# Products of a recurrence's decays on GpSimd, their normalisation queued behind a state update

## The chip, the cores and the metric

The kernel runs on one core of a Trainium2 chip. The metric is the time of one execution in microseconds. The engines are named as in the profile: PE (TensorE), DVE (VectorE), ACT (ScalarE), POOL (GpSimd), and SP, which here issues the DMAs.

## The reference

```python
state = np.zeros((B, H, D, D))            # B 4, H 8, S 768, D 40
for t in range(S):
    y[:, :, t] = einsum('bhd,bhde->bhe', rt, state)
    Sa = einsum('bhde,bhe->bhd', state, at)
    state_decay = state * wt[:, :, None, :] - einsum('bhd,bhe->bhde', Sa, bt)
    state = state_decay + einsum('bhd,bhe->bhde', vt, kt)
x = y as (B, S, H * D)
x = _moe_ref(x)      # 4 experts of causal attention, the top 2 of each position
x = _moe2_ref(x)     # a token mixer and a channel mixer
```

The change concerns the recurrence alone, and in it the decays `w`, which lie between 0.85 and 0.95. `_moe_ref` and `_moe2_ref` are left as they are.

## The kernel before

The recurrence (class `Rec`) is computed in chunks of 64 steps, 12 in all, which go in 6 pairs, numbered 0 to 5. The 32 heads lie in G = 11 groups of three heads with 40 partitions each, so that most tiles have 120 partitions.

For a pair of chunks `decay(p)` builds running products of the decays. Each chunk has two halves of 32 steps. The tile `pq` holds the products from the start of a half (`pt`) and those from its end (`qt`). Both are built by the same 31 multiplications (L164), each of 120x88 numbers and each reading what the one before has written. Then come the product of a whole half (`wp`, L166), its reciprocal (L168) and two multiplications that normalise `pt` and `qt` (L171). Two tiny products `f` for the state's decay run on GpSimd (L174, L176).

`scale(p)` multiplies `a` by `pt` (L182), issues the DMAs that spread `a` into `abd`, and multiplies the two halves of `kb` by `qt` (L186). `ptt(p, q)` has PE transpose `pt` (L265). `scores` multiplies blocks of `kb` and `abd` on PE and masks them on DVE (L210). From their diagonal blocks `solve(p)` inverts triangular matrices: a transpose into `tp` (L226), 31 steps of two dependent DVE operations (L235, L237), and a transpose into `xt` (L240). PE reads `xt` in `xz` (L302). `ds` updates the state in four pieces, whose last operation is on DVE (`ST`, L333).

The tiles `w` and `pq` exist once each: the decays of the next pair can be loaded only when those of this one have been read, and `pq` can be written only when the last reader of the pair before is done.

The order in the program is written out by hand. `first()` follows the list `FIRST`; each later chunk follows `EVEN` or `ODD`, in which a letter stands for a step (`S` the solve, `D` the decay of the pair after next, `M` its scaling). The solves and, for pairs 2 to 5, the decays are generators in a queue `s.bg`, from which `s.pump(n)` takes n steps after each step of the list. `tc.issue_after(x)` makes the scheduler put what is in it behind the instruction x on its engine. The scheduler then fixes the order on each engine.

Of the kernel before, what the change touches and what calls it, by code (L numbers as in the profile page):

```python
# [19 lines left out]
F32 = mybir.dt.float32  # L20
# [5 lines left out]
OP = mybir.AluOpType  # L26
AX = mybir.AxisListType
PSUM = bass.MemoryType.PSUM
G = 11
HP = 3  # L30
E = 40
FIRST = "p0 S p1 p2 k0 k1 k2 X L D M V q0 q1 q2"
SPIN = 28
PN = (1, 1)
EVEN = "m2 v0 h0 c0 z0 v1 c1 r0 c2 D v2 z2 x2 c3 m0 c4 x0 t2 z1 y0 x1 t1 c5 t0 h1 r1 r2 x3 y1 h2 c6 c7 k0 x5 c8 s0 c9 y2 x4 c10 c11 s2 d0 m1 S L d2 s1 k1 k2 d1"
ODD = "A z0 x0 v0 v1 z1 z2 r0 h0 x2 t0 m1 x1 m2 s0 v2 r1 y0 h1 m0 r2 M y1 p0 L p1 p2 h2 y2 x3 t1 t2 d0 s2 k0 x5 s1 k1 x4 d2 k2 d1"
QUADS = [(0, 4), (4, 8), (8, 11)]
# [15 lines left out]
def nheads(g):  # L53
    return 2 if g == G - 1 else 3
# [15 lines left out]
class Rec:  # L70
# [76 lines left out]
    def decay(s, p):  # L147
        nc, wk, t = s.nc, s.wk, s.T[p]

        pq = s.ek.tile([120, 2, G, 2, 64], F32, name="pq", bufs=1)
        wp = wk.tile([120, G, 2, 2], F32, name="wp")
        e = nc.vector
        pt, qt, n, x = pq[:, 0], pq[:, 1], 4 * G, 128 * G
        wv, pv, qv = (z.rearrange("p g c (h t) -> p (g c) h t", h=2) for z in (t["w"], pt, qt))

        def two(z, o, step):
            return bass.AP(tensor=z.tensor, offset=z.offset + o, ap=[z.ap[0], [step, 2], [32, n]])

        e.memset(two(pq, 0, x + 31), 1.0)  # L161
        for i in range(31):
            yield
            e.tensor_tensor(two(pq, i + 1, x + 29 - 2 * i), two(t["w"], i, 31 - 2 * i),  # L164
                            two(pq, i, x + 31 - 2 * i), OP.mult)
        e.tensor_tensor(wp.rearrange("p g c h -> p (g c) h"), wv[:, :, :, 31], pv[:, :, :, 31], OP.mult)  # L166
        wr = wk.tile([120, G, 2, 2], F32, name="wr")
        e.reciprocal(wr, wp)  # L168
        rv = wr.rearrange("p g c h -> p (g c) h")
        for z, h in ((pv, 0), (qv, 1)):  # L170
            e.tensor_tensor(z[:, :, h], z[:, :, h], rv[:, :, h:h + 1].to_broadcast([120, 2 * G, 32]), OP.mult)  # L171

        f = wk.tile([120, 2, G], F32, name="f")
        nc.gpsimd.tensor_tensor(f[:, 1, :], wp[:, :, 0, 1], wp[:, :, 1, 0], OP.mult)  # L174
        if p:
            nc.gpsimd.tensor_tensor(f[:, 0, :], s.T[p - 1]["wp"][:, :, 1, 1], wp[:, :, 0, 0], OP.mult)  # L176
        t.update(pt=pt, qt=qt, wp=wp, f=f)
# [130 lines left out]
    def ds(s, c, q, pre):  # L308

        nc = s.nc  # L310
        g0, g1 = QUADS[q]
        kbt, vu = s.T["kbt", c], s.T["vu", c]
        f = s.T[(c + 1) // 2]["f"][:, (c + 1) % 2]
        if pre:
            mf = s.wk.tile([120, 4, 120], F32, name="mf", bufs=3)
            for g in range(g0, g1):
                nc.scalar.activation(mf[:, g - g0], s.bdm, AF.Copy, scale=f[:, g:g + 1])
            s.T["mf", q] = mf
            return
        mf = s.T["mf", q]  # L320
        ps = s.ps.tile([128, 512], F32, name="pm")
        for g in range(g0, g1):
            k = 40 * nheads(g)
            o = 120 * (g - g0)
            nc.tensor.matmul(ps[:k, o:o + k], kbt[:, 120 * g:120 * g + k], vu[:, 120 * g:120 * g + k],  # L325
                             start=True, stop=False)
            nc.tensor.matmul(ps[:k, o:o + k], s.S[:k, g, :k], s.ident[:k, :k], is_transpose=True,
                             start=False, stop=True)
        for gg in ([(g0, g1)] if g1 < G else [(g0, g1 - 1), (g1 - 1, g1)]):
            k = 40 * nheads(gg[1] - 1)  # L330
            l, m = gg[0] - g0, gg[1] - g0
            pv = ps[:k, :480].rearrange("p (g d) -> p g d", d=120)[:, l:m, :k]
            nc.vector.tensor_tensor(s.ST[:k, gg[0]:gg[1], :k], pv, mf[:k, l:m, :k], OP.mult)  # L333

    def st(s, q):
        nc = s.nc
# [85 lines left out]
    def first(s):  # L422

        nc = s.nc
        s.load_w(0)
        s.load_a(0)
        kb = s.ek.tile([120, G, 2, 128], F32, name="kb")
        s.T[0]["kb"] = kb
        src = s.in_kb[0].rearrange("p g c x t -> p g c (x t)")
        for c in range(2):  # L430
            nc.sync.dma_start(kb[:, :, c], src[:, :, c])
        s.consts()
        s.bg = [s.decay(0)]
        s.pump(1000)
        t = s.T[0]
        a, p, q = t["a"], t["pt"], t["qt"]
        e = nc.vector
        for c in range(2):
            e.tensor_tensor(a[:, :, c], a[:, :, c], p[:, :, c], OP.mult)
            s.abd_load(c, (s.abd, s.rbd)[c][0])  # L440
            for x in range(2):
                kbx = kb[:, :, c, 64 * x:64 * x + 64]
                e.tensor_tensor(kbx, kbx, q[:, :, c], OP.mult)
        s.load_chunk(0)
        s.load_r(0)
        for c in range(2):
            for u in range(6):
                s.scores(c, u)

    def run(s):  # L450
        n = s.np
        s.first()

        def loads():
            s.load_w(1)
            s.load_a(1)
            s.load_kb(1)

        def all(f):
            for _ in f:  # L460
                pass

        def decay():
            with s.tc.issue_after(s.solved.ins):
                all(s.decay(1))

        do = dict(S=lambda: all(s.solve(0)), p=lambda q: s.ptt(0, q), L=loads, D=decay,
                  M=lambda: s.scale(1), q=lambda q: s.ptt(1, q), V=lambda: s.load_chunk(1),
                  k=lambda q: s.kbt(0, q), X=lambda: s.spin(s.T['sc', 1], SPIN))
        for o in FIRST.split():  # L470
            if n > 1 or o[0] not in "LDMq":
                do[o[0]](*map(int, o[1:]))
        s.bg = []
        for c in range(2 * n):
            s.chunk(c)
        with s.tc.issue_after(s.solved.ins):
            for _ in s.cv:
                pass
        for q in range(3):
            s.vut(2 * n - 1, q)  # L480
            s.rs(2 * n - 1, q)
            s.hh(2 * n - 1, q)
            s.yy(2 * n - 1, q)
# [9 lines left out]
    def chunk(s, c):  # L493
        n = s.np
        p = c // 2
# [47 lines left out]

        def decay():
            if even and p2:
                s.bg.append(s.decay(p + 2))

        def scale():
            if not even and p2:
                while "pt" not in s.T[p + 2]:  # L550
                    s.pump(1)
                s.scale(p + 2)

        if even and p2:
            s.load_w(p + 2)
# [596 lines left out]
```

## Time and profile before

| | us |
|---|---|
| median of 3 runs | 1045.84 (1043.87 to 1049.55) |
| profiled execution | 1045.46 |
| its span in the trace | 1043.7 |
| PE busy | 959.1 |
| DVE busy | 674.4 |
| ACT busy | 479.3 |
| GpSimd busy | 167.7 |

The span is what the trace covers; 1.8 us lie outside it. A busy time is the sum of an engine's instructions; one that is not the bound can be idle at no cost. The recurrence takes the first 410 us or so.

### The profile page before, as it was taken

How to read it: one execution, taken by the hardware profiler on the slowest of the kernel's cores; microseconds unless marked ns; L12 is line 12 of the kernel's file. 1: busy time of each engine (PE TensorE's matmuls, PEld its weight loads, DVE VectorE, ACT ScalarE, POOL GpSimd, SP SyncE). 2: the span in 40 equal slices, each digit the busy share in tenths (PEclk: the TensorE clock that was granted, in tenths of full speed). 3: DMA queues.
4: the chain of work that ended last, by engine and by line, in shares of the span. 5: the costliest groups of instructions: out<-in, count | busy, mean ns of one | idle time of the engine just before them, and what ended most of it. 6: DMA issues, size and time to landing. Idle time of an engine off the chain costs nothing.

```text
span 1043.7 us, 23515 instructions
## 1 busy us (share of the span) xinstructions
PE 959.1 (92%) x9313; PEld 823.1 (79%) x9313; DVE 674.4 (65%) x1793; ACT 479.3 (46%) x1250; POOL 167.7 (16%) x214
## 2 busy tenths in 40 slices
PE   2977997999999999966999999999998999999998
PEld 1646876888888898855877888888787898898987
DVE  6598898887989685747898777566287222222222
ACT  1324544656665665534677667666543121121211
POOL 5000000010000000352234132223255000000000
PEclk9977996999999999979999999999999999999999
DMA  8604422417253323455543441420262101101000
GB/s 172 138 1 96 100 67 74 111 41 170 53 123 74 86 61 117 157 165 145 154 116 99 118 115 31 96 65 26 87 205 63 56 1 56 39 18 57 1 26 26
DMA packets 101031, 88.84 MB, mean 85 GB/s; under 512 B 60785, under 2 KB 91073, under 8 KB 100321
## 3 DMA queue, kind: packets, MB, share of 16 engines
q1 hardware_dynamic: 100921, 87.34, 32.2%
q8 instruction: 74, 1.21, 0.5%
q14 instruction: 36, 0.29, 0.1%
HBM read 54.94 MB, written 15.73 MB: 68 GB/s over the span
## 4 chain that ended last, share of the span: by engine, by line
PE 66%; DVE 19%; DMA 6%; ACT 4%; issue 3%; POOL 1%; SPq 1%; DVEq 0%; ACTq 0%; POOLq 0%
PE pq L1045 12%; PE p L1059 11%; PE psc L205 4%; PE zu L289 3%; PE psc L387 3%; DVE pq L164 3%; PE po L872 3%; PE pq L846 3%; PE zu L302 2%; PE pq L998 2%; PE pm L325 2%; PE zu L276 2%; DVE x L237 2%; PE y L400 2%; DVE pr L235 2%
## 5 line engine op out<-in xcount | busy, mean ns | idle before, releaser
L1049 DVE SCALAR_TENSOR_TENSOR hl<-pq,hh 128x512 fp32r<-128x512 f32 x72 | 49.7, 690 | 153.6 <-ACT hh L1048 153.6
L1048 ACT ACTIVATE hh<-pq 128x512 fp32r<-128x512 f32 x72 | 42.9, 596 | 186.7 <-PE pq L1045 186.7
L1059 PE MATMUL p<-c2h,hh 128*128 128x320 f32 x288 | 90.8, 315 | 0.0
L819 ACT ACTIVATE a<-s,nm 128x512 f32<-128x512 f32 (+3 forms) x128 | 68.7, 542 | 46.4 <-DVE nm L816 21.6
L1059 PE MATMUL p<-c2l,hh 128*128 128x320 f32 x288 | 89.4, 311 | 0.2 <-POOL c2l L635 0.2
L1059 PE MATMUL p<-c2h,hl 128*128 128x320 f32 x288 | 89.5, 311 | 0.1
L306 ACT ACTIVATE vu<-zu 32x240 f32<-32x240 f32 (+1 forms) x144 | 48.8, 339 | 55.2 <-PE zu L302 45.1
L293 ACT ACTIVATE zt<-zu 32x240 f32<-32x240 f32 (+1 forms) x144 | 48.7, 338 | 51.7 <-PE zu L289 49.6
L814 DVE TENSOR_REDUCE nm<-s 128x1 f32<-128x512 f32 (+3 forms) x128 | 62.0, 500 | 15.7 <-PE s L813 10.8
L164 DVE TENSOR_TENSOR pq<-w,pq 120x88 f32<-120x88 f32 x186 | 61.2, 329 | 9.7 <-DMA w<-in_w 5.8
L832 POOL TENSOR_TENSOR a<-a,rs 128x128 f32<-128x128 f32 (+1 forms) x64 | 45.6, 734 | 126.6 <-DVE rs L827 84.5
L235 DVE TENSOR_TENSOR pr<-tp,x 128x31 f32<-128x31 f32 (+15 forms) x186 | 63.0, 339 | 3.8 <-DVE tp L226 0.5
L237 DVE TENSOR_TENSOR x<-x,pr 128x31 f32<-128x31 f32 (+15 forms) x186 | 63.2, 340 | 3.3
L289 PE MATMUL zu<-vu,sc 64*32 64x40 f32 (+1 forms) x1536 | 61.3, 220 | 1.2 <-ACT vu L306 1.2
L302 PE MATMUL zu<-zt,xt 64*32 64x40 f32 x1536 | 48.3, 211 | 12.5 <-DVE pq L161 6.8
L1045 PE MATMUL pq<-uh,c1h 128*128 128x512 f32 x144 | 57.6, 400 | 0.8 <-DVE ul L666 0.8
L289 PEld LDWEIGHTS zu<-vu,sc 64*32 64x32 f32 (+1 forms) x1536 | 53.2, 127 | 6.2 <-ACT vu L306 2.9
L1059 PEld LDWEIGHTS p<-c2h,hh 128*128 128x128 f32 x288 | 54.5, 189 | 3.7 <-DVE o L1062 1.2
L1045 PE MATMUL pq<-uh,c1l 128*128 128x512 f32 x144 | 57.1, 396 | 0.0
L1059 PEld LDWEIGHTS p<-c2l,hh 128*128 128x128 f32 x288 | 54.5, 189 | 2.9 <-POOL c2l L635 0.5
L387 PE MATMUL psc<-rbd,vut 120*128 120x192 f32 (+1 forms) x264 | 54.6, 341 | 1.9 <-DVE sr L391 1.6
L302 PEld LDWEIGHTS zu<-zt,xt 64*32 64x32 f32 x1536 | 40.3, 117 | 20.1 <-issue 12.8
(206 smaller groups left out, 2504.4 us busy)
## 6 DMA issues: line engine op xcount, KB each, us to landing
kb<-in_kb SPq DMA_DIRECT2D x5, 1320.0 KB
kh<-hb SPq DMA_DIRECT2D x64, 96.0 KB
cv<-in_c SPq DMA_DIRECT2D x18, 256.0 KB
w<-in_w SPq DMA_DIRECT2D x6, 660.0 KB
a<-in_a SPq DMA_DIRECT2D x6, 660.0 KB
r<-in_r SPq DMA_DIRECT2D x12, 330.0 KB
rbd<-in_r SPq DMA_DIRECT2D x36, 110.0 KB
vu<-in_v SPq DMA_DIRECT2D x12, 320.0 KB
```

Of the source, the lines that this page charges most:

```text
L164: e.tensor_tensor(two(pq, i + 1, x + 29 - 2 * i), two(t["w"], i, 31 - 2 * i), two(pq, i, x + 31 - 2 * i), OP.mult)
L235: v.tensor_tensor(prv, tp[:, j + 1:, j:j + 1].to_broadcast([128, n, j + 1]), x[:, j:j + 1, :j + 1].to_broadcast([128, n, j + 1]), OP.mult)
L237: v.tensor_tensor(x[:, j + 1:, :j + 1], x[:, j + 1:, :j + 1], prv, OP.subtract)
L289: nc.tensor.matmul(zu[o:o + m, 40 * i:40 * i + 40], sc[r, h, 32 * half:32 * half + m], vu[r, 40 * h:40 * h + 40], start=False, stop=True, ...
L302: nc.tensor.matmul(zu[o:o + 32, 240 + 40 * i:280 + 40 * i], xt[r, h, :], s.zt[half][r, 40 * h:40 * h + 40], start=True, stop=True, skip_gr ...
L306: nc.scalar.activation(vu[d:d + 32, o:o + n], zu[b + 32 * half:b + 32 * half + 32, 240:240 + n], AF.Copy)
L387: nc.tensor.matmul(ps[:, n:n + nheads(g), :], vt[:k, g - g0, :], rbd[:k, g, :nheads(g), :], start=True, stop=True)
L814: nc.vector.tensor_reduce(nm[:, x:x + 1], s, axis=AX.X, op=OP.max, negate=True)
L819: nc.scalar.activation(a[:, n0:n1], s, AF.Exp, bias=nm[:, -1:] if nb_ == 2 else nm[:, :1], accum_out=sm[:, x, i % 2:i % 2 + 1])
L1045: nc.tensor.matmul(p, l, r, start=(n == 0), stop=(n == 7))
L1049: nc.vector.scalar_tensor_tensor(hl, p, 0.0, hh, op0=OP.max, op1=OP.subtract)
L1059: nc.tensor.matmul(Y[s][i], hs[x][:, ts], w[:, k], start=(k + n == 0), stop=(k == 11 and n == 2))
```

## The change

For pairs 1 to 5 the memset of `pq` and the 31 products run on GpSimd; pair 0 keeps them on DVE. What followed them in `decay(p)` is a function of its own, `norm(p)`, still on DVE. For pair 1 the products are issued without a wait on the solve; `norm(1)` and `scale(1)` stand behind `xt` of the first solve, as the whole of `decay(1)` did. For pairs 2 to 5 the products are issued at once at `D`, not step by step, and `norm` and `scale` come at `M` in the odd chunk, behind the last state update of the even chunk (`s.moved`).

```diff
--- before.py
+++ after.py
@@ -150,19 +150,26 @@
         pq = s.ek.tile([120, 2, G, 2, 64], F32, name="pq", bufs=1)
-        wp = wk.tile([120, G, 2, 2], F32, name="wp")
-        e = nc.vector
-        pt, qt, n, x = pq[:, 0], pq[:, 1], 4 * G, 128 * G
-        wv, pv, qv = (z.rearrange("p g c (h t) -> p (g c) h t", h=2) for z in (t["w"], pt, qt))
+        e = nc.gpsimd if p else nc.vector
+        n, x = 4 * G, 128 * G
...
+        t["pq"] = pq
         e.memset(two(pq, 0, x + 31), 1.0)
         for i in range(31):
             yield
             e.tensor_tensor(two(pq, i + 1, x + 29 - 2 * i), two(t["w"], i, 31 - 2 * i),
                             two(pq, i, x + 31 - 2 * i), OP.mult)
+
+    def norm(s, p):
+        nc, wk, t = s.nc, s.wk, s.T[p]
+        pq = t["pq"]
+        wp = wk.tile([120, G, 2, 2], F32, name="wp")
+        e = nc.vector
+        pt, qt = pq[:, 0], pq[:, 1]
+        wv, pv, qv = (z.rearrange("p g c (h t) -> p (g c) h t", h=2) for z in (t["w"], pt, qt))
         e.tensor_tensor(wp.rearrange("p g c h -> p (g c) h"), wv[:, :, :, 31], pv[:, :, :, 31], OP.mult)
...
-            nc.vector.tensor_tensor(s.ST[:k, gg[0]:gg[1], :k], pv, mf[:k, l:m, :k], OP.mult)
+            s.moved = nc.vector.tensor_tensor(s.ST[:k, gg[0]:gg[1], :k], pv, mf[:k, l:m, :k], OP.mult)
...
         s.pump(1000)
+        s.norm(0)
...
         def decay():
+            all(s.decay(1))
+
+        def scale():
             with s.tc.issue_after(s.solved.ins):
-                all(s.decay(1))
+                s.norm(1)
+                s.scale(1)
...
-                  M=lambda: s.scale(1), q=lambda q: s.ptt(1, q), V=lambda: s.load_chunk(1),
+                  M=scale, q=lambda q: s.ptt(1, q), V=lambda: s.load_chunk(1),
...
         def decay():
             if even and p2:
-                s.bg.append(s.decay(p + 2))
+                for _ in s.decay(p + 2):
+                    pass
 
         def scale():
             if not even and p2:
-                while "pt" not in s.T[p + 2]:
-                    s.pump(1)
-                s.scale(p + 2)
+                with s.tc.issue_after(s.moved.ins):
+                    s.norm(p + 2)
+                    s.scale(p + 2)
```

Three places in the order of the engines. The first is DVE at the head, behind the first solve's `xt`: here the rows of before, from the normalisation of pair 1 on, where the products in them are already those of pair 2.

```order
L171 TENSOR_TENSOR pq<-pq,wr 120x22x32 x2
L182 TENSOR_TENSOR a<-a,pq 120x1408
L186 TENSOR_TENSOR kb<-kb,pq 120x22x64 x2
L161 MEMSET pq 120x2x44
L164 TENSOR_TENSOR pq<-w,pq 120x2x44
L333 TENSOR_TENSOR ST<-pm,mf 120x480
L164 TENSOR_TENSOR pq<-w,pq 120x2x44
L333 TENSOR_TENSOR ST<-pm,mf 120x240
L164 TENSOR_TENSOR pq<-w,pq 120x2x44
L333 TENSOR_TENSOR ST<-pm,mf 80x80
L164 TENSOR_TENSOR pq<-w,pq 120x2x44 x11
L333 TENSOR_TENSOR ST<-pm,mf 120x480
```

And the same place after the change (L247 is the line of `xt`, L173 to L178 are those of `norm`, L189 and L193 of `scale`, L340 of `ST`, L217 of the masked scores).

```order
L247 STREAM_TRANSPOSE xt<-x 128x32x32
L173 TENSOR_TENSOR wp<-w,pq 120x44
L175 RECIPROCAL wr<-wp 120x44
L178 TENSOR_TENSOR pq<-pq,wr 120x22x32 x2
L189 TENSOR_TENSOR a<-a,pq 120x1408
L193 TENSOR_TENSOR kb<-kb,pq 120x22x64 x2
L340 TENSOR_TENSOR ST<-pm,mf 120x480
L340 TENSOR_TENSOR ST<-pm,mf 120x240
L340 TENSOR_TENSOR ST<-pm,mf 80x80
L217 TENSOR_TENSOR sc<-psc,mask 128x384 x4
L340 TENSOR_TENSOR ST<-pm,mf 120x480
```

No product is left on DVE there: `xt` is followed by `wp`, and the state updates by scores.

The second place is DVE around the end of the solve of pair 1. Before:

```order
L237 TENSOR_TENSOR x<-x,pr 128x3x29
L210 TENSOR_TENSOR sc<-psc,mask 128x384
L235 TENSOR_TENSOR pr<-tp,x 128x60
L164 TENSOR_TENSOR pq<-w,pq 120x2x44
L237 TENSOR_TENSOR x<-x,pr 128x2x30
L210 TENSOR_TENSOR sc<-psc,mask 128x128
L235 TENSOR_TENSOR pr<-tp,x 128x31
L164 TENSOR_TENSOR pq<-w,pq 120x2x44
L237 TENSOR_TENSOR x<-x,pr 128x31
L166 TENSOR_TENSOR wp<-w,pq 120x44
L240 STREAM_TRANSPOSE xt<-x 128x32x32
```

And after (L242 and L244 are the two operations of a solve's step, L233 is the transpose `tp` of the next pair's solve).

```order
L242 TENSOR_TENSOR pr<-tp,x 128x60
L244 TENSOR_TENSOR x<-x,pr 128x2x30
L242 TENSOR_TENSOR pr<-tp,x 128x31
L244 TENSOR_TENSOR x<-x,pr 128x31
L233 STREAM_TRANSPOSE tp<-td 128x1024
L247 STREAM_TRANSPOSE xt<-x 128x32x32
L242 TENSOR_TENSOR pr<-tp,x 128x31
L244 TENSOR_TENSOR x<-x,pr 128x31
```

The products between the solve's operations are gone, and the next pair's `tp` stands ahead of `xt`; the scores lie earlier.

The third place is GpSimd after the change, from the `f` of pair 0 on, with what each row waits for (L160 and L163 are the memset of `pq` and the products, L130 a memset of `vu`, L235 and L236 those of the solve's `x`, L181 and L183 the `f`).

```order
L181 TENSOR_TENSOR f<-wp 120x11 [waits DVE_49]
L130 MEMSET vu 64x1280 [waits Pool_49]
L235 MEMSET x 128x1024 [waits Pool_49]
L130 MEMSET vu 64x1280
L236 MEMSET x 128x32 [waits Pool_49]
L160 MEMSET pq 120x2x44 [waits DVE_49,PE_49]
L163 TENSOR_TENSOR pq<-w,pq 120x2x44 [waits DMAHW6_49,Pool_49]
L163 TENSOR_TENSOR pq<-w,pq 120x2x44 [waits Pool_49] x30
L130 MEMSET vu 64x1280 [waits Pool_49]
L235 MEMSET x 128x1024 [waits DVE_49,Pool_49]
L181 TENSOR_TENSOR f<-wp 120x11 [waits DVE_49]
```

The products of pair 1 now stand on GpSimd behind the memsets for the first chunks, and wait for the readers of pair 0's `pq` and for the load of `w`.

## Rows read from the trace of the kernel before

**Rows 1.** The page, section 4: shares of the chain that ended last, by engine.

```profile
PE 66%; DVE 19%; DMA 6%; ACT 4%; issue 3%; POOL 1%; SPq 1%; DVEq 0%; ACTq 0%; POOLq 0%
PE pq L1045 12%; PE p L1059 11%; PE psc L205 4%; PE zu L289 3%; PE psc L387 3%; DVE pq L164 3%; PE po L872 3%; PE pq L846 3%; PE zu L302 2%; PE pq L998 2%; PE pm L325 2%; PE zu L276 2%; DVE x L237 2%; PE y L400 2%; DVE pr L235 2%
```

**Rows 2.** Waits of PE, total us, times, longest.

```profile
PE pm L265 <- DVE pq L171: 5.6, 1, 5.6
PE zu L302 <- DVE xt L240: 4.9, 3, 3.8
```

**Rows 3.** Busy time by stretch: start:end and length, then PE, PEld, DVE, ACT, POOL.

```profile
85.00:120.00 35.00, 33.72 (x442) 28.84 (x440) 29.99 (x62) 21.13 (x53) 1.54 (x3) 0.92 0.53 124
...
150.00:166.00 16.00, 7.69 (x55) 5.44 (x52) 15.68 (x53) 3.18 (x5) 0.39 (x2) 0.79 0.32 90
...
185.00:216.00 31.00, 29.71 (x462) 26.53 (x458) 27.63 (x75) 18.41 (x53) 2.32 (x2) 1.00 0.38 88
...
250.00:283.00 33.00, 31.38 (x439) 28.00 (x438) 29.14 (x82) 17.22 (x47) 2.32 (x2) 0.95 0.33 78
```

**Rows 4.** Timeline of DVE at the head: start, us, operation.

```profile
69.73 1.90 DVE L240 STREAM_TRANSPOSE xt<-x 128x1024 f32<-128x1024 f32 x1
...
71.81 11.17 DVE L164 TENSOR_TENSOR pq<-w,pq 120x88 f32<-120x88 f32 x31
...
85.36 1.62 DVE L182 TENSOR_TENSOR a<-a,pq 120x1408 f32<-120x1408 f32 x1
```

**Rows 5.** Timeline of PE at the head; in brackets idle time before and releaser.

```profile
76.96 2.10 PE L302 MATMUL zu<-zt,xt 64*32 64x40 f32 x47
84.70 2.52 PE L265 MATMUL pm<-ident,pq 120*128 120x120 f32 x11 [5.63 <-DVE pq L171]
```

**Rows 6.** Timeline of DVE between pair 0's scaling and the first solve.

```profile
23.47 1.69 DVE L443 TENSOR_TENSOR kb<-kb,pq 120x704 f32<-120x704 f32 x2
...
46.33 0.21 DVE L235 TENSOR_TENSOR pr<-tp,x 128x31 f32<-128x31 f32 x1 [0.50 <-DVE tp L226]
```

**Rows 7.** Two stretches behind PE's restart, as rows 3; the granted clock follows POOL.

```profile
85.00:91.00 6.00, 5.98 (x28) 4.85 (x27) 5.51 (x6) 3.21 (x7) 0.00 (x0) 0.51 0.62 152
91.00:94.00 3.00, 3.00 (x33) 2.71 (x32) 2.13 (x7) 1.39 (x5) 0.00 (x0) 1.00 0.02 6
```

**Rows 8.** Groups of DVE in 125 to 164.2: count, busy us, mean ns.

```profile
L164 DVE TENSOR_TENSOR pq<-w,pq 120x88 f32<-120x88 f32 x26 | 8.6, 331 | 0.0
```

**Rows 9.** Timeline of DVE near the end of pair 1's solve.

```profile
161.47 0.31 DVE L164 TENSOR_TENSOR pq<-w,pq 120x88 f32<-120x88 f32 x1
161.69 0.24 DVE L235 TENSOR_TENSOR pr<-tp,x 128x87 f32<-128x87 f32 x1
```

**Rows 10.** Groups of POOL by shape: count, busy us, mean ns.

```profile
L580 POOL TENSOR_TENSOR sc<-sc 128x512 f32<-128x512 f32 x6 | 8.0, 1331 | 48.7 <-DVE sc L579 47.4 <-PE y L357 1.3
...
L832 POOL TENSOR_TENSOR a<-a,rs 128x128 f32<-128x128 f32 x16 | 6.5, 409 | 82.9 <-DVE rs L827 69.6 <-ACT hb L781 5.2 <-ACT a L819 4.9
...
L174 POOL TENSOR_TENSOR f<-wp 120x11 f32<-120x11 f32 x6 | 1.2, 207 | 87.1 <-DVE wp L166 40.5 <-ACT zt L293 23.3 <-ACT S L348 12.3
```

**Rows 11.** Timeline of all engines where weights are split, behind the recurrence.

```profile
454.39 0.29 DVE L574 TENSOR_SCALAR cv<-cv 128x256 int32<-128x256 int32 x1 [2.02 <-DMA cv<-in_c]
...
454.73 2.08 POOL L635 TENSOR_TENSOR t1l<-cv,t1h 128x768 fp32r<-128x768 f32 x1 [2.76 <-ACT t1h L634]
...
455.17 1.78 DVE L577 TENSOR_SCALAR cv<-cv 128x256 int32<-128x256 int32 x1
...
457.45 0.49 DVE L666 TENSOR_TENSOR xl<-pq,xh 128x128 fp32r<-128x128 f32 x2
457.50 0.73 POOL L580 TENSOR_TENSOR cv<-cv 128x256 f32<-128x256 f32 x1 [0.69 <-DVE cv L579]
```

**Rows 12.** Groups of DVE in 170 to 214.7, most of pair 2's solve.

```profile
L164 DVE TENSOR_TENSOR pq<-w,pq 120x88 f32<-120x88 f32 x12 | 4.0, 335 | 0.0
```

**Rows 13.** Groups of DVE in 240 to 282.2, most of pair 3's solve.

```profile
L164 DVE TENSOR_TENSOR pq<-w,pq 120x88 f32<-120x88 f32 x13 | 4.3, 329 | 0.0
```

**Rows 14.** Timeline of PE at its first use of pair 3's xt.

```profile
284.30 1.09 PE L302 MATMUL zu<-zt,xt 64*32 64x40 f32 x42 [0.49 <-DVE pq L164]
```

## Prediction

> **What bounds the kernel now.** I read the chain that ended last first [rows 1]: PE holds 66% of it and DVE 19%, and the decay products of L164 appear in it under a name of their own with 3%. Next the list of what PE waits for [rows 2]: one wait of 5.6 us is on the normalised decays, and the waits on xt add up to 4.9 us. Then the stretches [rows 3]. In most of the recurrence PE is busy for nearly the whole stretch (29.71 of 31 us, 31.38 of 33). There are two places where it isn't: the head, where pair 1's decays are built, and 150 to 166, where PE works 7.69 of 16 us while DVE works 15.68. Everything behind 410 us is the mixture of experts and the channel mixer, which the change doesn't touch.
>
> So a microsecond taken off DVE is worth a microsecond in those two places, and little elsewhere until DVE falls behind.
>
> **The change part by part.**
>
> *Head.* Between the solve's transpose xt(0), which ends at 71.63, and the normalisation DVE spends 11.2 us on the 31 products of pair 1 [rows 4]. PE finishes its own work at 79.06 and sits idle to 84.70, released by the normalisation [rows 5]. After the change DVE goes from xt(0) straight to wp. From the last product to the end of the normalisation is 2.4 us (82.98 to 85.36), so PE's transposes could start at about 74, and PE has work until 79. The idle 5.6 us goes. GpSimd must have the products ready at 71.6. It may write pq only when the scaling of pair 0 has read it, by about 25 us, and until the solve begins at 46.3 DVE has only scores, whose input is in PSUM [rows 6]. With 13 us for the products (below) they end near 39, before the solve, and even at 22 us near 47. I cost them at nothing; without that cover they would slow the solve, as below.
>
> The idle stretch also has a price behind it. In 85:91 PE is busy throughout at half speed (a granted clock of 0.51), and from 91 it has full speed [rows 7]. If the idle stretch goes, the clock may be back before this work. Matmuls that are bound by the clock would then take half of the 6 us, a gain of 3.0 at most; nothing is the other end. I take 2.0, nearer the top since PE is busy throughout that row. Head: −7.6 us.
>
> *Products of pair 2.* They lie between the state updates and scores of 90 to 106; PE idles 1.3 us in 85:120 in all [rows 3]. I take −0.8 (0 to −1.3). GpSimd starts them when pair 1 is scaled, about 79 (w(2) can be loaded once wp of pair 1 has read w(1), near 72), and ends about 92; the normalisation stands on DVE behind the last state update, which DVE reaches at about 94. What is queued behind it are chunk 3's scores. The price of late products there is their lateness less the 5.0 us that DVE idles in 85:120 [rows 3].
>
> *Solve of pair 1* (the long DVE stretch to 166). Of the products 26 lie between 125 and 164 [rows 8]. One product between two solve operations costs the queue not its 0.33 us but what lies from its start to that of the next operation, 0.22 to 0.26 (161.47 to 161.69 [rows 9]), since they overlap: 26 × 0.245 = 6.4 us go. Against it, the next pair's transpose tp, which stands behind xt now, comes before it in the new order; as one of xt's kind it takes 1.9 us [rows 4]: +2.0.
>
> *What GpSimd's products do to DVE.* No row shows 120x88 on GpSimd. The bounds are a 120x11 product of 0.207 us and a 128x128 one of 0.409 [rows 10]; a line from the first to the second gives 0.34 at 88, one from the first to 128x512 (1.33) gives 0.38. I take 0.36, with 0.06 between dependent instructions: 13 us for 31, bounds 6.5 and 15 (22 if two runs of strided data cost as much again). The other price is that of meeting DVE. While GpSimd ran a 768-wide product for 2.08 us, a DVE operation on 128x256 took 1.78, where another of its kind and size just before took 0.29 [rows 11]: it waited for nearly all that was left of the product. Both read SBUF. Two DVE operations with an input in PSUM, just behind, take 0.49 together beside a product of GpSimd, and don't look stretched. The solve's two operations per step, the scaling and the normalisation have all inputs in SBUF. If each product that meets the solve holds back one operation, it costs 0.36 − 0.06 = 0.30 us. The Trainium skill says so outright ("SBUF — State Buffer", section "Who interferes with whom"): a VectorE instruction with two SBUF inputs and a GpSimd instruction that reads SBUF exclude each other, and the second one is fully blocked. By it the price is the 0.30 taken here; if GpSimd were free of DVE, the price would be nothing. The trace's pair of 2.08 and 1.78 us agrees with the page.
>
> Pair 3's products run on GpSimd from about 108 to 121, and meet the solve of pair 1 in their last 11: +3.3 (0 to +5). The solve of pair 1 thus comes to −6.4 + 2.0 + 3.3 = −1.1 (−4.4 to +0.6).
>
> *Solves of pairs 2 and 3.* Here 12 and 13 products lie between solve operations [rows 12] and [rows 13]; without them −6.1 us together. But GpSimd's products for the next pair now start when the earlier scaling has let go of pq, and fall on the solve: I count 22 meetings in the one (it is one third over) and all 31 in the other: 53 × 0.30 = +15.9. DVE is idle 3.4 us of 31 and 3.9 of 33 [rows 3], which takes up some: 15.9 − 6.1 − 7.3 = +2.5 us. That the rest is felt at once is in the rows: PE takes up xt(3) at 284.30, having waited 0.49 us for DVE [rows 14]. I take +3.0, for what doesn't spread evenly; bounds 0 (products of 0.21 us: 53 × 0.15 = 8, less than 13.4) and +5 (products of 0.41). In pair 4 no products are left, and the normalisation and scaling come into the solve: nothing.
>
> *Moved.* The normalisation and scaling are queued behind the even chunk's last state update, not among the pumped steps; their 2.3 and 4.8 us on DVE are the same. The load of w(4) moves behind kb(3) on SP, 60 us ahead of its use. Both nothing.
>
> **Sum.** −7.6 − 0.8 − 1.1 + 3.0 = −6.5 us on the profiled execution's 1045.46 gives 1039.0; that execution is 0.4 below the median of the runs.
>
> **Rivals.**
> - *No contention* (chance 0.20): GpSimd and DVE don't hinder each other here. For it: no row shows these shapes together. Against: the stretched operation of [rows 11]. Then the solve of pair 1 is −4.4, pairs 2 and 3 nothing: −7.6 − 0.8 − 4.4 = −12.8, or 1032.7.
> - *The gain is eaten* (0.22): products near 0.45 us. The meetings cost 53 × 0.39 = 20.7, less 13.4 is +7.3; pair 1 +0.6. −7.6 − 0.8 + 0.6 + 7.3 = −0.5, or 1045.0: no change that can be told.
> - *GpSimd becomes the bound* (0.13): strided products take 0.6 us or more. Then pairs 2 and 3 pay 53 × 0.54 = 28.6 less 13.4 = +15.2, PE waiting at both xt, and the solve of pair 1 +1: −7.6 − 0.8 + 1.0 + 15.2 = +7.8, or 1053.3. It decides from 0.48 us for a product, where the meetings eat the head's gain. For it: the products' rows are of one run each, and these have strides and two runs. Against: the 120x11 form is strided too and costs 0.207; at the 2.6 ns an element of the 1.33 us form, 88 elements add 0.23 to that.
> - *The forecast* (0.45): 1039.0.
>
> **How the numbers follow.** About 0.5%, 5.2 us, is what measurement can tell. The forecast's own range is 1035 to 1042; the range over the cases, 1030 to 1048, leaves out most of the third rival and the far end of the first. Faster by over 0.5% (under 1040.6): all of the first rival, 0.36 of the forecast's 0.45, little of the second: 0.58. Same: 0.28. Slower: 0.14.
>
> **What would show it.** After the change: PE has no wait on the normalised decays near 80, and the clock is at full speed before 85 (head). xt(1) ends near 156, with a wait before L302 of some 3 us left. A GpSimd product takes 0.34 to 0.37 us, more where it meets the solve; the solve's operations have means above 0.34 us in pairs 2 and 3, and PE waits 1 to 4 us for xt(2) or xt(3). Wrong would be: solve operations of unchanged means (first rival), products of 0.5 us and more (third), or a normalisation on DVE that waits for GpSimd.

## The result, and the profile after

The changed kernel takes 1056.62 us in the median of 16 runs (1043.22 to 1064.09), the kernel before 1044.55. The ratio is 1.0079 (1.0055 to 1.0102): 0.8% slower, where 0.6% faster was forecast and the range ended at 1048. It leaves out the slowest five of the 16 runs; the two medians by themselves lie 1.2% apart. The profiled execution has a span of 1052.7 us.

First the engines' busy times and the GpSimd products on the page of the changed kernel (L163 is their line).

```profile
PE 970.1 (92%) x9313; PEld 829.5 (79%) x9313; DVE 644.8 (61%) x1633; ACT 480.9 (46%) x1250; POOL 250.2 (24%) x374
...
L163 POOL TENSOR_TENSOR pq<-w,pq 120x88 f32<-120x88 f32 x155 | 80.1, 517 | 12.5 <-DMA w<-in_w 0.4
```

DVE lost 30 us of work and GpSimd gained 82. PE has exactly as many matmuls as before and is busy 11 us longer (959.1 before): the same matmuls took longer. The span less this busy time is 84.6 us before and 82.6 after, so in this pair of executions all of the 9 us is longer matmuls and none of it more waiting. A product on GpSimd takes 0.517 us, not 0.36. Next the waits of PE on DVE that answer to [rows 2].

```profile
PE zu L309 <- DVE xt L247: 8.4, 4, 7.0
PE zu L309 <- DVE wp L173: 6.9, 1, 6.9
PE y L364 <- DVE ptt L411: 3.8, 2, 2.8
```

The 5.6 us on the normalised decays are gone, as forecast. The waits for xt, 4.9 us before, are 8.4, and 7.0 of that is xt(1) (3.8 before), which was to be early. The 6.9 us under `wp` are the wait for xt(0), put down to the operation that DVE does next; before, the same 6.8 us stand under the memset of `pq`, so [rows 2] leaves them out. Now the stretches, as in [rows 3] and [rows 7].

```profile
72.00:79.00 7.00, 7.00 (x95) 5.58 (x95) 4.44 (x3) 3.89 (x10) 2.13 (x5) 0.50 0.50 111
...
85.00:88.00 3.00, 3.00 (x18) 3.00 (x17) 0.66 (x1) 0.66 (x4) 2.61 (x6) 0.50 0.00 0
88.00:91.00 3.00, 3.00 (x23) 2.16 (x21) 0.55 (x2) 1.86 (x5) 2.61 (x6) 0.77 0.04 8
...
352.00:365.00 13.00, 13.00 (x129) 10.84 (x122) 2.99 (x6) 4.70 (x14) 0.00 (x0) 0.51 0.48 96
```

At the head PE now works from 69.7 us without a wait longer than 0.43 us, yet at half speed until about 89. Before, it waited 5.6 us there and had full speed from 91; in both the clock came back 19 to 20 us after PE took up xt(0). And behind xt(4) there are 13 us of full work at half speed, a stretch that the trace of before has at full speed (its mean granted clock from 342 to 375 is 1.00). By half of the 13 us, an estimate, about 6.5 us are lost there alone. Where it begins, PE's timeline shows this.

```profile
345.97 0.57 PE L349 MATMUL pm<-ident,ST 120*120 120x120 f32 x4
347.20 0.42 PE L349 MATMUL pm<-ident,ST 120*120 120x120 f32 x2 [0.66 <-ACT S L355]
...
349.50 0.69 PE L309 MATMUL zu<-zt,xt 64*32 64x40 f32 x21 [0.45 <-DVE xt L247]
350.85 0.51 PE L296 MATMUL zu<-vu,sc 64*32 64x40 f32 x13 [0.31 <-ACT vu L313]
```

Three short waits follow one another, for ACT, for xt(4) and again for ACT. In the order of before PE had only the waits of 0.43 and 0.31 us there; the 0.66 us is new, and matmuls of scores and outputs that stood behind xt(4) now lie ahead of it.

Why is xt(4) late? From tp(4) at 300.60 to xt(4) at 347.50 are 46.9 us, against 40.5 before (300.26 to 340.80), though no product is left in this solve. DVE's timeline shows the new entries.

```profile
308.67 0.33 DVE L244 TENSOR_TENSOR x<-x,pr 128x175 f32<-128x175 f32 x1
311.50 1.63 DVE L193 TENSOR_TENSOR kb<-kb,pq 120x1408 f32<-120x1408 f32 x1 [2.50 <-DMA kb<-in_kb]
...
347.50 1.95 DVE L247 STREAM_TRANSPOSE xt<-x 128x1024 f32<-128x1024 f32 x1
349.48 0.66 DVE L411 TENSOR_TENSOR ptt<-y,ptt 64x240 f32<-64x240 f32 x2
```

The normalisation of pair 5 stood ahead of tp(4) before; now it lies in the solve, 2.3 us. The whole solve stands behind the scaling, which waits 2.50 us for the load of kb (1.24 before). And the scheduler has put one `sc`, four `sr` and four `ptt` operations ahead of xt(4) that came behind it before.

Last, the run-to-run spread. The 16 runs of the changed kernel lie between 1043.2 us at a mean granted clock of 0.969 and 1064.1 at 0.948, on a line of 8.6 us per 0.01 (a fit over the 16). The median clock is 0.956; that of 91 runs of the kernel before, made with the experiments below, is 0.965. At 0.965 the line gives 1048.9 us, and the like line of before 1045.2. So of 11.6 us between the medians of all these runs some 8 go with the lower granted clock, and 4 are the rest.

### The profile page after: what moved, and what is told of

The parts are those of the page before. It is cut to its first block, busy times and chain, and to the rows that moved or that the text cites. A ratio compares the mean times of both kernels' runs of the same rounds, so it can differ in the third digit from the quotient of the medians.

```text
span 1052.7 us, 23516 instructions
## 1 busy us (share of the span) xinstructions
PE 970.1 (92%) x9313; PEld 829.5 (79%) x9313; DVE 644.8 (61%) x1633; ACT 480.9 (46%) x1250; POOL 250.2 (24%) x374
## 4 chain that ended last, share of the span: by engine, by line
PE 66%; DVE 18%; DMA 7%; ACT 5%; issue 3%; POOL 1%; SPq 1%; DVEq 0%; ACTq 0%; POOLq 0%
PE pq L1058 11%; PE p L1072 11%; PE psc L212 5%; PE psc L394 3%; PE zu L309 3%; PE zu L296 3%; PE pq L859 3%; PE po L885 3%; DVE pr L242 3%; DVE x L244 2%; PE pm L332 2%; PE pq L1011 2%; PE y L407 2%; DMA kb<-in_kb 2%; PE pq L1024 2%
## 5 line engine op out<-in xcount | busy, mean ns | idle before, releaser
L163 POOL TENSOR_TENSOR pq<-w,pq 120x88 f32<-120x88 f32 x155 | 80.1, 517 | 12.5 <-DMA w<-in_w 0.4
L313 ACT ACTIVATE vu<-zu 32x240 f32<-32x240 f32 (+1 forms) x144 | 48.9, 339 | 56.0 <-PE zu L309 52.1
L827 DVE TENSOR_REDUCE nm<-s 128x1 f32<-128x512 f32 (+3 forms) x128 | 62.0, 500 | 15.9 <-PE s L826 11.6
L242 DVE TENSOR_TENSOR pr<-tp,x 128x31 f32<-128x31 f32 (+15 forms) x186 | 67.7, 364 | 5.8 <-POOL x L236 1.3
L244 DVE TENSOR_TENSOR x<-x,pr 128x31 f32<-128x31 f32 (+15 forms) x186 | 67.4, 362 | 3.9
L217 DVE TENSOR_TENSOR sc<-psc,mask 128x384 f32<-128x384 f32 x72 | 36.0, 511 | 47.2 <-PE psc L212 45.9
L309 PE MATMUL zu<-zt,xt 64*32 64x40 f32 x1536 | 49.9, 214 | 15.8 <-DVE xt L247 8.4
L309 PEld LDWEIGHTS zu<-zt,xt 64*32 64x32 f32 x1536 | 41.2, 119 | 26.0 <-issue 14.6
```

The lines of the kernel that those rows point to most:

```text
L242: v.tensor_tensor(prv, tp[:, j + 1:, j:j + 1].to_broadcast([128, n, j + 1]), x[:, j:j + 1, :j + 1].to_broadcast([128, n, j + 1]), OP.mult)
L244: v.tensor_tensor(x[:, j + 1:, :j + 1], x[:, j + 1:, :j + 1], prv, OP.subtract)
L309: nc.tensor.matmul(zu[o:o + 32, 240 + 40 * i:280 + 40 * i], xt[r, h, :], s.zt[half][r, 40 * h:40 * h + 40], start=True, stop=True, skip_gr ...
L313: nc.scalar.activation(vu[d:d + 32, o:o + n], zu[b + 32 * half:b + 32 * half + 32, 240:240 + n], AF.Copy)
L827: nc.vector.tensor_reduce(nm[:, x:x + 1], s, axis=AX.X, op=OP.max, negate=True)
```

## Experiments

The theories. **A**: short waits of PE around xt, which the new order makes, are followed by stretches at half speed. **B**: GpSimd's products hold up the solves, and that is all. **C**: the shift at the head brings the loss. **D**: the stretches at half speed have nothing to do with those waits. **E**, later: the place of the normalisation and scaling makes the loss. All ratios are to the kernel before in the same job.

| run | median us | ratio (95%) | median clock |
|---|---|---|---|
| e1_pair1_only | 1035.21 | 0.9924 (0.9893 to 0.9955) | 0.966 |
| e2_pairs2to5_only | 1079.67 | 1.0279 (1.0221 to 1.0337) | 0.945 |
| e3_norm_place_only | 1050.36 | 1.0059 (1.0031 to 1.0088) | 0.958 |
| e4_ones | 1054.59 | 1.0100 (1.0066 to 1.0133) | 0.954 |
| f1_after_fill | 1069.45 | 1.0213 (1.0167 to 1.0259) | 0.960 |
| f2_e1_spin34 | 1045.01 | 0.9990 (0.9961 to 1.0018) | 0.966 |
| f4_e1_fill | 1052.75 | 1.0058 (1.0025 to 1.0090) | 0.966 |
| g1_pair1_and_norm | 1063.06 | 1.0168 (1.0114 to 1.0221) | 0.948 |
| i1_e1_dummy | 1045.30 | 1.0009 (0.9979 to 1.0039) | 0.960 |
| h1_e1_act | 1037.22 | 0.9933 (0.9918 to 0.9947) | 0.968 |
| h3_pairs12 | 1035.04 | 0.9920 (0.9894 to 0.9945) | 0.968 |
| i2_e1_memset | 1037.78 | 0.9909 (0.9883 to 0.9934) | 0.966 |
| k1_norm5 | 1044.42 | 0.9990 (0.9965 to 1.0014) | 0.960 |
| k3_norm3 | 1040.69 | 0.9965 (0.9937 to 0.9992) | 0.965 |

**The change in two halves.** First only pair 1 in the new way. `GP` holds the pairs whose products run on GpSimd; the others have products, normalisation and scaling as before.

```diff
+GP = (1,)
-        e = nc.gpsimd if p else nc.vector
+        e = nc.gpsimd if p in GP else nc.vector
...
+        if p and p not in GP:
+            s.norm(p)
...
+                if p + 2 not in GP:
+                    s.bg.append(s.decay(p + 2))
+                    return
...
+                if p + 2 not in GP:
+                    while "pt" not in s.T[p + 2]:
+                        s.pump(1)
+                    return s.scale(p + 2)
```

> Only pair 1's products are on GpSimd, pairs 2 to 5 as before. Theory A (the clock: the time that the head frees is worked off at half speed, and the extra time comes from more PE work at half speed wherever DVE falls behind): the head's idle 5.6 us goes, the clock still comes back near 90, so 0 to -4 us against before, 1041 to 1045, and little more half-speed work behind the head. Theory B (contention of GpSimd's products with the solves of pairs 2 and 3 is the whole loss): -5 to -8 us, 1037 to 1040. Theory C (the shift at the head itself brings on the later falls of the clock): as slow as the full change, about 1055.

0.8% faster, 1035.21 us: theory B's size or a little more, and the fastest version but for an equal one below. C falls. So moving pair 1 is worth what the prediction said of the head, and pairs 2 to 5 cost about twice that.

Then the other half, `GP = (2, 3, 4, 5)`.

> Pair 1 as before, pairs 2 to 5 as in the change. Theory A: xt(3) and xt(4) later by 5 to 8 us against before, and a stretch at half speed behind one of them that before doesn't have: +6 to +14 us, 1051 to 1058. Theory B: +8 to +12 us with the granted clock as before. Theory C: within 3 us of before.

2.8% slower, more than any theory said. A wait that the full change just escapes is in it: pair 1's products are on DVE again, so pq is released late. The timeline of GpSimd shows when pair 2's products begin:

```profile
86.39 17.56 POOL L164 TENSOR_TENSOR pq<-w,pq 120x88 f32<-120x88 f32 x31
```

And the list of PE's waits has a new entry, in chunk 3's scores:

```profile
PE psc L215 <- DVE sc L220: 10.2, 1, 10.2
```

The products end at 103.9. The normalisation waits for them on DVE, chunk 3's scores stand behind it, and PE waits 10.2 us for those. This is the price of a late product that the prediction named for this place; in the full change they end at 94.5, ahead of the normalisation at 97.5.

**The place of the normalisation alone.** All products on DVE step by step, normalisation and scaling of pairs 2 to 5 behind the state update.

```diff
+        s.done = p
...
-                while "pt" not in s.T[p + 2]:
-                    s.pump(1)
-                s.scale(p + 2)
+                while s.done != p + 2:
+                    s.pump(1)
+                with s.tc.issue_after(s.moved.ins):
+                    s.norm(p + 2)
+                    s.scale(p + 2)
```

> All products on DVE, stepwise as before; only the normalisation and scaling of pairs 2 to 5 stand behind the even chunk's last state update. If the place of the normalisation and scaling in the solves (with a wait for kb, as in 308 to 311 us of the changed kernel) makes the loss: +4 to +8 us. If GpSimd's products make it, by contention or the clock: within 3 us of before.

0.6% slower with no product on GpSimd, at the size of the first theory. The prediction had costed this move at nothing. But what the changed kernel showed around xt(4) repeats here only in part. From tp(4) to xt(4) are 47.0 us, as long as there, the scaling waits 2.59 us for the load of kb, and PE's timeline shows the same three waits:

```profile
340.31 0.42 PE L353 MATMUL pm<-ident,ST 120*120 120x120 f32 x2 [0.66 <-ACT S L359]
...
342.61 1.04 PE L313 MATMUL zu<-zt,xt 64*32 64x40 f32 x40 [0.45 <-DVE xt L251]
343.96 0.51 PE L300 MATMUL zu<-vu,sc 64*32 64x40 f32 x13 [0.31 <-ACT vu L317]
```

Yet the stretch behind them has full speed:

```profile
343.00:360.00 17.00, 16.69 (x293) 14.02 (x291) 9.31 (x22) 12.70 (x33) 0.79 (x2) 1.00 0.44 98
```

In this trace the fall comes behind xt(5), in 395 to 412, behind waits of 0.64 and 0.31 us.

**The changed order without its products.**

```diff
+        if p > 1:
+            e.memset(pq, 1.0)
+            return
         e.memset(two(pq, 0, x + 31), 1.0)
```

> The changed kernel in the same order, but for pairs 2 to 5 the 31 products are left out: GpSimd only sets pq to ones, so that it reads nothing beside the solves (the decays of those pairs are then missing from the result). If GpSimd's products against DVE make the loss (A or B): the solve's operations are back at a mean of 0.340 us, xt(3) and xt(4) come 4 to 8 us earlier than in the changed kernel, 1036 to 1044. If it is the place of the normalisation or the head: 1050 or more, the granted clock near 0.957.

The instructions stand in the order of the changed kernel, GpSimd reads nothing beside the solves of pairs 2 to 5, and the solve's operations are back at 337 and 334 ns (the two groups in the solve of pair 3; 398 and 389 in the changed kernel).

```profile
L247 DVE TENSOR_TENSOR x<-x,pr 128x31 f32<-128x31 f32 (+15 forms) x31 | 10.5, 337 | 0.5
L245 DVE TENSOR_TENSOR pr<-tp,x 128x31 f32<-128x31 f32 (+15 forms) x31 | 10.4, 334 | 0.4
```

Yet it is 1.0% slower than before; the interval overlaps that of the full change. B falls as the sole cause. In the view of stretches there are three at half speed: in 281 to 292, in 346 to 364, and behind xt(5) this one of 16 us:

```profile
404.00:420.00 16.00, 16.00 (x224) 14.13 (x225) 5.77 (x13) 7.07 (x20) 2.53 (x2) 0.50 0.19 58
```

**The clock and the waits.** Two matmuls that nobody reads, in the wait behind the first group of L309, in the changed kernel and in the one with pair 1 alone.

```diff
             do[o[0]](int(o[1:] or 0))
+            if even and c and o == "x0":
+                s.spin(s.T["xt", p], 2)
```

> The changed kernel, and in the even chunks of pairs 1 to 5 two matmuls of 128x512 whose result nobody reads, behind the first group of L309, where PE waits 0.31 us for ACT. They are 0.86 us of PE work each time, some 3 us in all beyond the waits. Theory A (the changed order leaves PE with short waits around xt, behind which the clock falls in some executions): fewer falls there, the granted clock up to 0.963 or more, and the median at 1043 to 1052 in spite of the added work. Theory D (the falls have nothing to do with those waits): the median at 1058 to 1060.

> The same two matmuls in the kernel with only pair 1's products on GpSimd. Theory A: few falls are there to be saved, so 0 to +4 us against that kernel without them, 1035 to 1039. Theory D: +3 to +5 us, 1038 to 1040.

In the trace each added matmul is two instructions of 0.44 us (12 take 5.31 us in the next timeline), 20 in the five places, so 8.8 us were added, twice what these expectations took. Both kernels lose more than that, 13 us and 17 us, and the median clock hardly moves (0.956 to 0.960, and 0.966 both times). They tell A and D apart badly: they also changed the order around them and took a turn of the two `pm` buffers. What they show is that matmuls put into that place aren't free. One hint for A is in the trace of the first: PE waits 1.39, 1.48 and 1.17 us for xt(3), xt(4) and xt(5), and the falls there last some 4 us each (293 to 297, 361 to 365, 416 to 420), with a clock of 1.00 in the 7 us behind each. That is one execution.

Then the head: PE kept busy up to xt(0), with `SPIN = 34` for 28.

> Only pair 1's products on GpSimd, and at the head 12 more of the matmuls that keep PE busy during the first solve (34 in place of 28), about 5 us of PE work, in time in which PE waits for xt(0). If the head's half-speed stretch behind xt(0) follows from that wait: the clock stays at full speed there, PE works the 18 us behind it in less, and the median comes to 1027 to 1032. If not: 1035 as without them, or more if they run past xt(0).

1045.01, so 10 us lost, not 5 gained. The scheduler now put the transposes of pair 1's decays ahead of the products with xt(0), as PE's timeline shows:

```profile
61.71 5.31 PE L512 MATMUL pm<-sc,ident 128*128 128x512 f32 x12
70.91 1.01 PE L275 MATMUL pm<-ident,pq 120*128 120x120 f32 x8 [3.89 <-DVE pq L181]
```

The view of stretches has the clock right behind that wait:

```profile
72.00:74.00 2.00, 2.00 (x29) 1.55 (x28) 2.00 (x2) 1.60 (x5) 0.00 (x0) 0.51 0.75 169
```

The wait came back as one for the normalised decays (3.89 us), and the clock fell at 72 instead of 66. The head's half-speed stretch stayed.

Last, ACT copies twice, so that PE should wait longer.

```diff
-        for b, o, n in spans(q):
+        for b, o, n in spans(q) * (2 if c in (4, 6, 8, 10) and (q, half) == (0, 0) else 1):
```

> Only pair 1's products on GpSimd; in the first group of L309 of pairs 2 to 5 ACT does its two copies to vu twice, so that PE waits some 0.7 us longer there, four times. Theory A (short waits of PE around xt are what the falls of the clock follow): more than the waits themselves, +6 to +14 us against 1035, the granted clock at 0.960 or lower. If only the waits count: 0 to +3 us and a clock of 0.966.

PE's wait there is 0.31 us as before, so the second copies were hidden: the run doesn't test A.

**Placement again, with the head.** Pair 1 on GpSimd, pairs 2 to 5 as in the run on the normalisation's place.

> Pair 1's products on GpSimd; pairs 2 to 5 with products on DVE step by step, normalisation and scaling behind the even chunk's last state update. It differs from the full change only in where the products of pairs 2 to 5 run. If the place of the normalisation makes most of the loss by falls of the clock: 1042 to 1050, a granted clock below 0.962. If the products of pairs 2 to 5 on GpSimd do: 1035 to 1038.

1.7% slower than before and 2.4% slower than with pair 1 alone, from which it differs only by the place of normalisation and scaling. It is slower than the full change, too. Theory E holds; the products' engine in pairs 2 to 5 isn't needed for the loss. The same move costs 6 us without pair 1's change and 25 with it, and the median clocks are 0.958 and 0.948; why it costs so much more here isn't shown. What the time is lost in is on the pages, here with pair 1 alone, in a span of 1033.6 us:

```profile
PE 958.1 (93%) x9313; PEld 823.3 (80%) x9313; DVE 664.4 (64%) x1761; ACT 480.2 (46%) x1250; POOL 185.3 (18%) x246
```

And with the moved normalisation, in a span of 1057.1 us:

```profile
PE 978.5 (93%) x9313; PEld 836.4 (79%) x9313; DVE 659.9 (62%) x1761; ACT 480.4 (45%) x1250; POOL 184.4 (17%) x246
```

Of 23.5 us between the two executions 20.4 are longer matmuls, the same in number, and 3.1 more waiting of PE.

One pair at a time: pair 5 alone moved, and pair 3 alone. The other pairs are normalised right behind their products, as before; for pair 5:

```diff
+        if p in (2, 3, 4):
+            s.norm(p)
+        s.done = p
...
+                if "pt" in s.T[p + 2]:
+                    return s.scale(p + 2)
```

> Only pair 1's products on GpSimd, and the normalisation and scaling of pair 5 alone behind the state update, in the solve of pair 4. If each such move costs by itself: +3 to +9 us against 1035, with falls of the clock behind xt(4), near 330 us. If the loss needs the moves of several pairs: within 2 us.

> The same with pair 3 alone, whose normalisation and scaling then lie in the solve of pair 2, with tp(2) moved ahead of xt(1). If each such move costs by itself: +3 to +9 us against 1035, with falls of the clock behind xt(2), near 215 us, or behind xt(1). If the loss lies in later pairs: within 2 us.

9 and 5 us are lost against 1035.2 (7 and 4 by the ratios). So one move is enough in pair 5; for pair 3 the intervals of the two ratios overlap. In the run with pair 5 moved, PE's timeline around xt(4):

```profile
336.73 0.89 PE L411 MATMUL y<-kbt,sr 128*64 128x40 f32 x22
337.56 0.52 PE L353 MATMUL pm<-ident,ST 120*120 120x120 f32 x3
338.74 0.49 PE L353 MATMUL pm<-ident,ST 120*120 120x120 f32 x3 [0.66 <-ACT S L359]
340.07 1.04 PE L313 MATMUL zu<-zt,xt 64*32 64x40 f32 x40 [0.84 <-DVE xt L251]
341.42 0.51 PE L300 MATMUL zu<-vu,sc 64*32 64x40 f32 x13 [0.31 <-ACT vu L317]
```

And the stretch behind it, with its granted clock of 0.50:

```profile
342.00:358.00 16.00, 16.00 (x181) 13.42 (x174) 3.57 (x8) 6.09 (x18) 0.00 (x0) 0.50 0.22 63
```

PE's timeline at the same place with pair 1 alone:

```profile
329.34 0.82 PE L397 MATMUL psc<-rbd,vut 120*128 120x192 f32 x4
329.99 0.57 PE L262 MATMUL pm<-ident,kb 120*128 120x120 f32 x4
330.99 1.02 PE L312 MATMUL zu<-zt,xt 64*32 64x40 f32 x40 [0.42 <-DVE xt L250]
332.31 0.51 PE L299 MATMUL zu<-vu,sc 64*32 64x40 f32 x13 [0.31 <-ACT vu L316]
```

There the stretch that holds it has a clock of 1.00:

```profile
328.00:345.00 17.00, 16.27 (x327) 13.77 (x324) 9.28 (x20) 9.68 (x23) 1.12 (x2) 1.00 0.19 43
```

Moving the normalisation put xt(4) behind more of the scores and outputs in DVE's order (tp(4) to xt(4): 50.2 us against 40.1), and PE's outputs (L411) and last transposes ahead of L313. PE waits 1.81 us in three pieces instead of 0.73 in two, and then works 16 us at half speed instead of at full. By half of the 16, an estimate, that is 8 us behind waits that grew by 1. A second stretch at half speed, from 308 to 315, stands behind a wait of 2.22 us for DVE at 305.96 that the run with pair 1 alone doesn't have. In the run with pair 3 moved the clock's fall is elsewhere, in 393 to 407, behind xt(5), a place that the move didn't touch.

**Contention by itself.** With pair 1 alone on GpSimd, in an unchanged order on the other engines, GpSimd also computes products that nobody uses.

```diff
+        for i in range(31):
+            wa = bass.AP(tensor=w.tensor, offset=w.offset + i, ap=[w.ap[0], [31 - 2 * i, 2], [32, n]])
+            nc.gpsimd.tensor_tensor(y, wa, y, OP.mult)
```

> Only pair 1's products on GpSimd, the order on PE, DVE, ACT and SP unchanged against that kernel; in addition, for each of pairs 2 to 5, 31 dependent products of 120x88 on GpSimd that read w and a tile of their own and that nobody uses. They have the size and the reading of the real ones and run beside DVE. Theory B (contention of such products with the solves makes the loss of the full change): +8 us or more against 1035. Theory E (the order that follows from the place of normalisation and scaling makes it): 0 to +4 us, 1035 to 1039, granted clock 0.963 or more.

> As the run with dummy products, but each of the 31 is a memset of 120x88 on GpSimd, which writes and reads nothing. Order on PE, DVE, ACT and SP unchanged. If reading beside DVE is what costs: solve operations at a mean of 0.339 us again and 1034 to 1038. If any work of GpSimd there costs (its queue, the clock): 1041 to 1048.

10 us are lost with products and 2.6 with memsets, whose ratio is no worse than that without either. The memsets, which wait for no load, ran ahead of 65 us, so the second run is the same program with nothing beside the solves; it doesn't tell reading from writing. The groups of the solve's operations between 226 and 279 us, first with products:

```profile
L257 DVE TENSOR_TENSOR pr<-tp,x 128x31 f32<-128x31 f32 (+15 forms) x31 | 12.0, 387 | 0.3
L259 DVE TENSOR_TENSOR x<-x,pr 128x31 f32<-128x31 f32 (+15 forms) x31 | 12.0, 386 | 0.4
```

Then with memsets:

```profile
L259 DVE TENSOR_TENSOR x<-x,pr 128x31 f32<-128x31 f32 (+15 forms) x31 | 10.4, 337 | 0.4
L257 DVE TENSOR_TENSOR pr<-tp,x 128x31 f32<-128x31 f32 (+15 forms) x31 | 10.4, 336 | 0.3
```

3.2 us more in one solve. So contention is real, and costs 7 to 10 us in this order, part of it as lower clock (0.960 against 0.966). In the order of the change, which loses without it, it added nothing that can be told.

The same waits need not bring the fall. Around xt(5) PE's timeline with the unused products:

```profile
398.12 1.02 PE L324 MATMUL zu<-zt,xt 64*32 64x40 f32 x40 [0.62 <-DVE xt L262]
399.44 0.51 PE L311 MATMUL zu<-vu,sc 64*32 64x40 f32 x13 [0.31 <-ACT vu L328]
```

It reads as that with pair 1 alone:

```profile
386.18 1.02 PE L312 MATMUL zu<-zt,xt 64*32 64x40 f32 x40 [0.64 <-DVE xt L250]
387.50 0.51 PE L299 MATMUL zu<-vu,sc 64*32 64x40 f32 x13 [0.31 <-ACT vu L316]
```

But of the 12 us that follow, the stretch with the unused products is at half speed:

```profile
401.00:413.00 12.00, 12.00 (x151) 10.22 (x151) 4.26 (x10) 5.61 (x16) 2.53 (x2) 0.50 0.09 22
```

And that with pair 1 alone at full speed:

```profile
389.00:401.00 12.00, 11.76 (x204) 10.10 (x205) 5.53 (x13) 7.06 (x19) 2.54 (x2) 1.00 0.47 124
```

**Where GpSimd is free.** Pairs 1 and 2 in the new way, `GP = (1, 2)`.

> Pairs 1 and 2 in the new way, pairs 3 to 5 as before. Pair 2's normalisation stands ahead of chunk 3's scores, with GpSimd's products of 0.5 us each ending just ahead of it. If the loss lies in pairs 3 to 5 alone: 1033 to 1037. If pair 2 has a share: 1038 to 1045.

1035.04 us, as with pair 1 alone: pair 2's products end ahead of their normalisation and meet no solve, and the normalisation there moves nothing in the solves. This and the first run beat both kernels.

## Why the prediction was wrong

- **Moved: "Both nothing."** This is the step that failed. It counted the 2.3 and 4.8 us of normalisation and scaling as the same wherever they stand, and "In pair 4 ... nothing" with them. Placed in the solve they delay xt, put the solve behind a longer wait for kb (2.50 us for 1.24), and reorder PE: 6 us when done alone, 25 us (1.0168 less 0.9924, of 1045) on top of pair 1's change, most of it, in the two traces, as longer matmuls.
- **Head, −7.6: right in sum, in part by luck.** Pair 1 alone gives −8 us (−11 to −5 by its interval), and PE's wait of 5.6 us on the decays is gone. But in the traces only 5.0 us of it lie between xt(0) and xt(1), which start 94.5 us apart before and 89.5 with pair 1 alone; where the rest comes from isn't shown. The 2.0 us for the clock were for a wrong reason: it came back as long after xt(0) as before, though PE had hardly a gap, and not ahead of 85.
- **Products of pair 2, −0.8: too small to tell.** Moving them gained nothing that the runs can show (1035.04 against 1035.21). In the changed kernel they ended 3 us before the normalisation needed them, where 2 were forecast.
- **Solve of pair 1, −1.1 and an end near 156: wrong in place.** xt(1) started 3.5 us earlier than before, 2.1 of which were there at xt(0), and ended at 162.6. Its steps are queued among scores that PE hands over late, so DVE waits for PE in the solve (3.2 us in all); taking 26 products out of it shortened nothing (44.6 us from tp to xt, 41.0 before). It is 41.5 with pair 1 alone, where the products stand in it, and 41.7 in the run without products: +0.2 where −6.4 + 2.0 were forecast. With GpSimd's products it is 2.9 more (44.6), near the 3.3 forecast.
- **A product of 0.36 us: mis-sized.** 0.49 with nothing beside it, a pitch of 0.57, and 0.56 beside a solve. It was above the 0.48 at which the third rival was to decide. That this rival's 1053.3 lies near the 1054.46 of the profiled execution is chance: with no product in pairs 2 to 5 the loss is as large, so it came another way.
- **A meeting of 0.30 us: mis-sized the other way.** The 62 operations of pair 3's solve took 24.4 us, with 31 products beside some of them, where they took 20.8: 0.12 a product. The long wait beside a 2 us product [rows 11] doesn't scale down to this; its operation has one tensor input, the solve's have two, so that pair was no witness for them. So the +3.0 for the solves of pairs 2 and 3 had a wrong price in it, and its size can't be read off by itself.
- **The clock behind the head: not in the sum.** No term and no rival had PE's clock fall in pairs 2 to 5. By the fit over the runs it goes with the larger part of the loss, some 8 of 11.6 us.

What stays open: what decides whether the clock falls behind such a wait. The long falls behind xt in these traces follow short waits of PE (0.73 us in all in the run with memsets, 1.81 with pair 5 moved), but the same waits also pass without one, those of the changed kernel at xt(4) in the run on the normalisation's place. Theory A fits the order of events and is not shown as a cause; the two tries at it (more matmuls, more waiting) didn't isolate it. A rival is untested: that the order of before is a good one by its tuning, and that leaving it costs, whatever is moved. The added matmuls and the longer spin at the head also lost more than their own work.

## What to carry to other kernels

Take work off an engine only where another waits for it, here at the head: the edit gained 8 us for pair 1, and carried on to pairs 2 to 5 it lost 16. An instruction that is moved "for free" into another chain's queue delays that chain's end and reorders the engine that waits for it, so look at which instruction comes last there, not at the sum. Where a busy engine's total rises with the same instructions, read the granted clock by stretch before looking for a new wait, and time it in many runs.

## What the runs showed of the hardware that was not expected

- Short waits of PE can be followed by far longer stretches at half clock: 16 us of unbroken work behind waits of 1.81 us in all, in the run with pair 5 moved. It isn't so each time: the same 0.66, 0.45 and 0.31 us came ahead of 13 us at half clock in the changed kernel and of 17 us at full clock in the run on the normalisation's place.
- Continuous work doesn't bring the clock back at once: at the head of the changed kernel PE was busy from 69.7 but for two short gaps (0.1 and 0.43 us) and had half speed to about 89.
- The 120x88 f32 product on GpSimd takes 0.49 us, more than 128x128 with a broadcast operand (0.41), and 0.57 from one to the next when each needs the last.
- GpSimd's product and DVE's operation with two inputs in SBUF slow each other and don't shut each other out for the whole instruction. While products ran in the solve of pair 3, DVE's operations took up to 0.6 us instead of 0.4 and started 0.65 us apart (the rows below), and the 31 products took 19.7 us in all, 0.56 us each instead of 0.49. The Trainium skill ("SBUF — State Buffer", section "Summary: rules for kernel authors") says that the second one to issue is fully blocked until the first finishes. Were it so, a pair of them would take some 0.9 us, their sum. The measurement decides: both run, each slower.

The rows of the last point, from DVE's timeline of the changed kernel, first beside products:

```profile
263.13 0.61 DVE L242 TENSOR_TENSOR pr<-tp,x 128x255 f32<-128x255 f32 x1
263.78 0.60 DVE L244 TENSOR_TENSOR x<-x,pr 128x255 f32<-128x255 f32 x1
```

And in the next solve, where GpSimd has none:

```profile
326.39 0.41 DVE L244 TENSOR_TENSOR x<-x,pr 128x255 f32<-128x255 f32 x1
```
